# One batch's up-projection and the next attention on TensorE: an order written out by hand

## The chip, the cores and the metric

The kernel runs on one core of a Trainium2 chip. The metric is the device time of one execution in microseconds, the median of several. TensorE (PE in the rows) multiplies matrices; VectorE (DVE), ScalarE (ACT) and GpSimd (POOL) work on elements; SyncE (SP) issues most of the transfers. Each engine takes its instructions in the order that the program gives it.

## The reference

Three layers follow each other. Here they are, cut to what is computed:

```python
def reference(q, k, v, cap, w_in, w_out, w_gate, w1, w2):   # q, k, v: 4 x 12 x 448 x 64
    scores = q @ k.T / 8
    scores = cap * tanh(scores / cap)                       # cap = 30
    attn = softmax(scores) @ v
    x = attn as 1792 x 768                                  # 4 batches of 448 tokens
    g = relu(x @ w_in) ** 2                                 # 768 -> 2048
    x = g @ w_out                                           # 2048 -> 768
    # then each token goes to one of 8 experts, 224 tokens each, by greedy choice on x @ w_gate
    out[tokens of e] = relu(x[tokens of e] @ w1[e]) @ w2[e]
```

The weights w_in and w_out come as 64-bit integers' bits and are decoded on the chip.

## The kernel before, in words

The four batches are worked one after the other, and the attention of a batch runs beside the projections of the batch ahead of it. `merge` takes steps from several generators: each step says how much time it is worth, and the generator that is least far along by its own total goes next. So the program writes down a merged order of `hidden(0)` (up-projection of batch 0) with `attention(1)`; then `output(0)` and `hidden(1)` with `attention(2)`, and so on.

That written order is only a suggestion where a scheduler places the instructions: it may move an instruction ahead of others when its model of the engines finds it ready first. Inside `manual_schedule(engines={PE})` TensorE keeps the written order. Before the change this holds from `attention(2)` on, and not for `attention(0)`, nor for the merge of `hidden(0)` with `attention(1)`.

Attention of a batch goes through six head pairs, 0 to 5. For a head pair there are four blocks of keys: three pairs of 64-row score products (line 233), of which the two halves run at the same time, and one full product (L235). ScalarE takes tanh and exp (L237, L238). The value products are three pairs (L258) and one full product (L261) into one accumulator "aux". The sums of the exponentials, z, are added up block by block (L244, L246, L250): on VectorE for batch 0, on GpSimd for the others. The norm is a pair of products of z with ones (L266); then VectorE adds a small number (L268; ScalarE for later batches), takes the reciprocal (L269) and multiplies (L271), which gives x. `split_rows` splits x in a high part xh (L315, ScalarE) and a low part xl (L316, VectorE).

`hidden` makes 16 tiles of 128 features. A tile is 18 products, three for each of the six head pairs' x: xh with the high weights (L395), xl with the high weights (L396), xh with the low weights (L397). Its accumulator "acc" has two buffers. Behind it ScalarE takes relu, square and a cast (L402 to L406), and VectorE or GpSimd a subtraction (L407). The weights of a tile are loaded, decoded by three VectorE operations (L328 to L330), cast (L356) and split (L357, mostly GpSimd); there are three buffers each for decoded, high and low weights. `output` works alike (L452 to L454).

With `whole` false, attention yields after each group of score or value products, so others may come between them. With `whole` true (batches 2 and 3) a step holds two score blocks, or all value products of a head pair and its norm.

Of the kernel before, what the change touches and what calls it, by code (L numbers as in the profile page):

```python
# [79 lines left out]
class Kernel:  # L80
# [5 lines left out]
    def run(self):  # L86
        tc = self.tc
        PS = bass.MemoryType.PSUM
        with tc.tile_pool(name="keep", bufs=1) as self.keep, \
                tc.tile_pool(name="wts", bufs=1) as self.wts, \  # L90
                tc.tile_pool(name="psum", bufs=2, space=PS) as self.psum, \
                tc.tile_pool(name="dram", bufs=1, space=bass.MemoryType.DRAM) as self.dram, \
                ExitStack() as right, ExitStack() as left:
            self.setup()
            self.mp = right.enter_context(tc.tile_pool(name="moe1", bufs=1, side="right"))
            self.gpool = self.mp
            xs = right.enter_context(ExitStack())
            self.xp = xs.enter_context(tc.tile_pool(name="x", bufs=ND, side="right"))
            with tc.tile_pool(name="x32", bufs=ND, side="right") as self.xq:
                with tc.tile_pool(name="rows", bufs=ND + 1, side="right") as self.tp, \  # L100
                        tc.tile_pool(name="attn", bufs=2, side="right") as self.ap:
                    merge([(self.attention(0), 44.0)])
                    self.split_rows(0)
                    merge([(self.hidden(0), 58.0), (self.attention(1), 44.0)])
                    for b in range(2, NB):
                        self.split_rows(b - 1)
                        streams = [(chain(self.output(b - 2), self.hidden(b - 1)), 118.0), (self.attention(b), 44.0)]
                        if b == NB - 1:
                            streams.append((self.gate_decode(), 30.0))
                        with tc.manual_schedule(engines={mybir.EngineType.PE}):  # L110
                            merge(streams)
                self.split_rows(NB - 1)
            self.gp = left.enter_context(tc.tile_pool(name="gate", bufs=1))
            last = left.enter_context(ExitStack())
            self.gpool = last.enter_context(tc.tile_pool(name="last", bufs=1))
            with tc.tile_pool(name="gate_load", bufs=5, side="right") as self.gl:
                with tc.manual_schedule(engines={mybir.EngineType.PE}):
                    merge([(self.hidden(NB - 1), 60.0), (self.gate_weights(), 80.0)])
            xs.close()
            self.tp = right.enter_context(tc.tile_pool(name="rows2", bufs=2, side="right"))  # L120
            self.rp = right.enter_context(tc.tile_pool(name="route", bufs=1, side="right"))
            self.router_setup()

            def room():
                last.close()
                self.ep = left.enter_context(tc.tile_pool(name="expert", bufs=2))

            with tc.manual_schedule(engines={mybir.EngineType.PE}):
                self.second(room)
# [76 lines left out]
    def attention(self, b):  # L206
# [13 lines left out]
        def load_v(hp):  # L220
            vt[hp] = ap.tile([128, KB + 1, 2 * DH], F32, name="v", bufs=3)
            nc.sync.dma_start(vt[hp], self.v[b, hp])
# [55 lines left out]
        load(0)  # L278
        load(1)
        load_v(0)  # L280
        whole = b > 1
        for hp in range(HP + 1):
            if hp < HP:
                if hp + 2 < HP:
# [613 lines left out]
def merge(streams):  # L898
    live = [[g, 0.0, total] for g, total in streams]
    while live:  # L900
        s = min(live, key=lambda x: x[1] / x[2])
        try:
            s[1] += next(s[0])
        except StopIteration:
            live.remove(s)
# [46 lines left out]
```

## Time and profile before

| | |
|---|---|
| median of 3 runs | 1101.09 us (1098.07 to 1101.76) |
| the profiled execution, its own time | 1098.67 us |
| its span | 1096.8 us |
| TensorE busy with products | 1063.3 us (97%) |
| VectorE busy | 676.2 us (62%) |
| ScalarE busy | 543.8 us (50%) |
| GpSimd busy | 351.0 us (32%) |

A row of the timeline gives the start, the duration, the engine, the line, the operation with its tiles and shapes, and in brackets the idle time ahead of it with what ended it. Products overlap, so the distance from one start to the next tells more than the duration. A 64-row product pair shows as x4, since each fp32 product is recorded in two passes. The granted clock is 1.00 at TensorE's upper level.

### The profile page before, as it was taken

What the parts mean: (1) busy time and instruction counts of PE and PEld (TensorE: products, weight loads), DVE (VectorE), ACT (ScalarE), POOL (GpSimd) and SP (SyncE); (2) the same over time, 40 slices, a digit from 0 to 9 for tenths busy, and PEclk for the clock granted to TensorE, in tenths of its full rate; (3) what the DMA queues carried; (4) which work ended last, traced back from release to release, by engine and by line L of the source; (5) the groups of instructions that cost most, each with busy time, mean ns of one, the idle gap of its engine ahead of it and who ended that gap; (6) DMA issues with size and microseconds to landing.
All of it is one profiled execution on the core that took longest, in us unless ns stands there. A gap on an engine that the chain in (4) does not pass through costs nothing.

```text
span 1096.8 us, 15959 instructions
## 1 busy us (share of the span) xinstructions
PE 1063.3 (97%) x5866; PEld 836.7 (76%) x5866; DVE 676.2 (62%) x1124; ACT 543.8 (50%) x843; POOL 351.0 (32%) x245
## 2 busy tenths in 40 slices
PE   6999999999999999999999999999899999999997
PEld 2336655776677677677787888888799899999996
DVE  5987999978545478788411355565666554555551
ACT  5876776444776744676654222222222223554551
POOL 0127776655221322221443444444210201220000
PEclk9999999999999999999999999999899999999999
DMA  7533655566533377765563233336472465965530
GB/s 278 195 117 124 218 187 203 184 237 232 158 100 95 95 226 245 251 223 200 183 213 95 67 95 103 94 104 213 153 279 70 153 215 179 307 216 185 200 111 26
DMA packets 79454, 187.20 MB, mean 171 GB/s; under 512 B 8528, under 2 KB 19312, under 8 KB 79376
## 3 DMA queue, kind: packets, MB, share of 16 engines
q1 hardware_dynamic: 64736, 169.24, 46.0%
q0 software_dynamic: 3424, 11.19, 3.4%
q10 hardware_dynamic: 11216, 5.75, 2.0%
q8 instruction: 46, 0.75, 0.3%
q14 instruction: 32, 0.26, 0.1%
HBM read 156.26 MB, written 29.88 MB: 170 GB/s over the span
## 4 chain that ended last, share of the span: by engine, by line
PE 65%; issue 12%; DVE 10%; DMA 8%; ACT 2%; POOL 1%; SPq 1%; POOLq 0%; DVEq 0%; ACTq 0%
PE big L877 6%; PE acc L395 6%; PE acc L452 6%; PE acc L396 6%; PE acc L397 6%; PE acc L454 5%; PE acc L453 5%; PE acc L839 5%; PE aux L258 3%; PE big L233 3%; DMA raw<-w_out 3%; PE aux L653 2%; DVE wf L329 2%; DVE wf L328 2%; PE acc L846 2%
## 5 line engine op out<-in xcount | busy, mean ns | idle before, releaser
L356 ACT CAST wh<-wf 128x512 fp32r<-128x512 f32 (+1 forms) x187 | 135.2, 723 | 268.5 <-PE acc L453 102.2
L357 POOL TENSOR_TENSOR wl<-wf,wh 128x512 fp32r<-128x512 f32 (+1 forms) x97 | 156.5, 1616 | 206.5 <-ACT wh L356 196.9
L395 PE MATMUL acc<-xh,wh 128*128 128x448 f32 x384 | 148.6, 389 | 2.0 <-ACT r L402 2.0
L452 PE MATMUL acc<-g,wh 128*128 128x448 f32 x384 | 150.4, 392 | 0.0
L396 PE MATMUL acc<-xl,wh 128*128 128x448 f32 x384 | 141.2, 368 | 1.9 <-DVE xl L316 1.9
L454 PE MATMUL acc<-g,wl 128*128 128x448 f32 x384 | 140.4, 366 | 1.2 <-DVE wl L357 1.2
L397 PE MATMUL acc<-xh,wl 128*128 128x448 f32 x384 | 140.4, 366 | 0.1
L453 PE MATMUL acc<-g,wh 128*128 128x448 f32 x384 | 139.9, 364 | 0.0
L357 DVE TENSOR_TENSOR wl<-wf,wh 128x768 fp32r<-128x768 f32 (+1 forms) x90 | 88.0, 979 | 61.1 <-ACT wh L356 60.3
L877 PE MATMUL big<-wh,g 128*112 128x384 f32 x512 | 117.8, 342 | 0.0
L237 ACT ACTIVATE p<-big,isc 128x896 f32<-128x896 f32 x96 | 85.7, 907 | 26.9 <-PE big L233 26.7
L395 PEld LDWEIGHTS acc<-xh,wh 128*128 128x128 f32 x384 | 72.1, 189 | 35.1 <-issue 15.7
L238 ACT ACTIVATE p<-p,capt 128x896 f32<-128x896 f32 x96 | 89.4, 949 | 1.3
L756 POOL DMA_INDIRECT xg<-x,idx x32 | 34.2, 1068 | 169.9 <-PE acc L775 93.3
L877 PEld LDWEIGHTS big<-wh,g 128*112 128x112 f32 x512 | 86.8, 175 | 0.8
L407 DVE TENSOR_TENSOR g<-r,g 128x448 fp32r<-128x448 f32 x58 | 49.4, 851 | 60.2 <-ACT g L406 57.6
L246 POOL TENSOR_TENSOR z<-z,p 128x896 f32<-128x896 f32 x18 | 38.9, 2162 | 146.4 <-ACT p L238 144.1
L452 PEld LDWEIGHTS acc<-g,wh 128*128 128x128 f32 x384 | 72.4, 189 | 14.4 <-issue 9.6
L396 PEld LDWEIGHTS acc<-xl,wh 128*128 128x128 f32 x384 | 72.6, 189 | 12.4 <-issue 4.1
L269 DVE RECIPROCAL d<-d 128x448 f32<-128x448 f32 x24 | 70.7, 2948 | 16.6 <-ACT d L268 16.5
L233 PE MATMUL big<-qk 64*128 64x448 f32 x288 | 74.1, 598 | 6.9 <-DMA qk<-qk 6.2
L454 PEld LDWEIGHTS acc<-g,wl 128*128 128x128 f32 x384 | 72.0, 187 | 9.4 <-DVE wl L357 2.7
(182 smaller groups left out, 1941.7 us busy)
## 6 DMA issues: line engine op xcount, KB each, us to landing
g<-w SPq DMA_DIRECT2D x68, 384.0 KB
wf<-wi SPq DMA_DIRECT2D x48, 384.0 KB
wf<-wo SPq DMA_DIRECT2D x72, 256.0 KB
wf<-w SPq DMA_DIRECT2D x36, 384.0 KB
raw<-w_in SPq DMA_DIRECT2D x16, 768.0 KB
raw<-w_out SPq DMA_DIRECT2D x24, 512.0 KB
raw<-w_out_t SPq DMA_DIRECT2D x24, 512.0 KB
wt<-wt SPq DMA_DIRECT2D x48, 256.0 KB
```

Of the source, the lines that this page charges most:

```text
L233: nc.tensor.matmul(ps[:, s, :S], k[rows], q[rows], start=True, stop=True)
L237: nc.scalar.activation(p, ps[:, :n, :S], AF.Tanh, scale=self.isc)
L238: e = nc.scalar.activation(p, p, AF.Exp, scale=self.capt)
L356: nc.scalar.copy(wh[:, :w], wf[:, :w])
L357: low.tensor_sub(wl[:, :w], wf[:, :w], wh[:, :w].bitcast(F32))
L395: nc.tensor.matmul(ps, wh[:, d], xh, start=(d == 0), stop=False)
L396: nc.tensor.matmul(ps, wh[:, d], xl, start=False, stop=False)
L397: nc.tensor.matmul(ps, wl[:, d], xh, start=False, stop=(d == ND - 1))
L452: nc.tensor.matmul(ps, a, gh, start=(f == 0), stop=False)
L453: nc.tensor.matmul(ps, a, gl, start=False, stop=False)
L454: nc.tensor.matmul(ps, z, gh, start=False, stop=(f == NF - 1))
L877: nc.tensor.matmul(acc[h][:, s, :DM // 2], l, r[:, s * (DM // 2):(s + 1) * (DM // 2)], start=(j == 0 and first), stop=(j == NF2 - 1 and last))
```

## The change

The merge of `hidden(0)` with `attention(1)` is put inside `manual_schedule` for TensorE, and `whole` becomes true for batch 1 as well.

```diff
                     self.split_rows(0)
-                    merge([(self.hidden(0), 58.0), (self.attention(1), 44.0)])
+                    with tc.manual_schedule(engines={mybir.EngineType.PE}):
+                        merge([(self.hidden(0), 58.0), (self.attention(1), 44.0)])
...
-        whole = b > 1
+        whole = b > 0
```

The new order's line numbers are one higher from line 104 on. The first place is TensorE's order at the end of the first attention. z_335 is the sum of head pair 5, xh_399 and xl_400 are x of head pair 4, xh_403 and xl_404 of head pair 5; acc_455 and acc_530 are tiles 0 and 1 before, acc_457 and acc_532 after; qk_467 and aux_573 belong to the second attention (head pairs 1 and 0). Before:

```order
L266 MATMUL aux_375<-z_335,ones_68 64x448
L395 MATMUL acc_455<-xh_399,wh_419 128x448
L395 MATMUL acc_530<-xh_399,wh_431 128x448
L266 MATMUL aux_375<-z_335,ones_68 64x448
L396 MATMUL acc_455<-xl_400,wh_419 128x448
L397 MATMUL acc_455<-xh_399,wl_420 128x448
L396 MATMUL acc_530<-xl_400,wh_431 128x448
L397 MATMUL acc_530<-xh_399,wl_432 128x448
L233 MATMUL big_544<-qk_467 128x448 x2
L233 MATMUL big_550<-qk_467 128x448 x2
L258 MATMUL aux_573<-p2_478,v_469 64x448 x2
L258 MATMUL aux_573<-p2_484,v_469 64x448 x2
```

And the same place on TensorE in the new order, where qk_467 is head pair 0 of the second attention:

```order
L267 MATMUL aux_375<-z_335,ones_68 64x448
L396 MATMUL acc_457<-xh_399,wh_421 128x448
L267 MATMUL aux_375<-z_335,ones_68 64x448
L397 MATMUL acc_457<-xl_400,wh_421 128x448
L398 MATMUL acc_457<-xh_399,wl_422 128x448
L396 MATMUL acc_457<-xh_403,wh_421 128x448
L397 MATMUL acc_457<-xl_404,wh_421 128x448
L398 MATMUL acc_457<-xh_403,wl_422 128x448
L234 MATMUL big_506<-qk_467 128x448 x2
L236 MATMUL big_513<-qk_467 128x448
L396 MATMUL acc_532<-xh_383,wh_433 128x448
```

Tile 1 has moved behind tile 0, and the second attention's next scores and value products have moved behind the products on x of head pair 5.

The second place is TensorE at the value products of head pair 2 of the second attention, aux_876 before and aux_878 after, with z_695 its sum. Before:

```order
L258 MATMUL aux_876<-p2_712,v_542 64x448 x2
L395 MATMUL acc_866<-xh_395,wh_745 128x448
L396 MATMUL acc_866<-xl_396,wh_745 128x448
L397 MATMUL acc_866<-xh_395,wl_746 128x448
L395 MATMUL acc_866<-xh_399,wh_745 128x448
L396 MATMUL acc_866<-xl_400,wh_745 128x448
L397 MATMUL acc_866<-xh_399,wl_746 128x448
L395 MATMUL acc_866<-xh_403,wh_745 128x448
L396 MATMUL acc_866<-xl_404,wh_745 128x448
L397 MATMUL acc_866<-xh_403,wl_746 128x448
L258 MATMUL aux_876<-p2_810,v_542 64x448 x2
L261 MATMUL aux_876<-p1_816,v_542 128x448
```

And the same place in TensorE's new order:

```order
L259 MATMUL aux_878<-p2_686,v_544 64x448 x2
L259 MATMUL aux_878<-p2_692,v_544 64x448 x2
L259 MATMUL aux_878<-p2_812,v_544 64x448 x2
L262 MATMUL aux_878<-p1_818,v_544 128x448
L267 MATMUL aux_886<-z_695,ones_68 64x448 x2
L396 MATMUL acc_868<-xh_395,wh_758 128x448
```

The projection products no longer stand between the value products, and the norm has moved directly behind them.

The third place is GpSimd's order around the sums of the same head pair, z_715 before and z_695 after; the wl rows split the weights of a tile. Before:

```order
L244 TENSOR_TENSOR z_715<-p2_684,p2_712 128x896
L357 TENSOR_TENSOR wl_627<-wf_578,wh_626 128x768
L407 TENSOR_TENSOR g_667<-r_664,g_667 128x448
L357 TENSOR_TENSOR wl_746<-wf_687,wh_745 128x768
L357 TENSOR_TENSOR wl_794<-wf_737,wh_793 128x768
L246 TENSOR_TENSOR z_715<-z_715,p2_810 128x896
L250 TENSOR_TENSOR z_715<-z_715,p1_816 64x448 x2
```

And in GpSimd's new order:

```order
L245 TENSOR_TENSOR z_695<-p2_686,p2_692 128x896
L358 TENSOR_TENSOR wl_759<-wf_697,wh_758 128x768
L358 TENSOR_TENSOR wl_796<-wf_750,wh_795 128x768
L247 TENSOR_TENSOR z_695<-z_695,p2_812 128x896
L358 TENSOR_TENSOR wl_865<-wf_787,wh_864 128x768
L251 TENSOR_TENSOR z_695<-z_695,p1_818 64x448 x2
```

A weight split has moved in between the last two sums.

## Rows read from the trace of the kernel before

**Rows 1.** Stretches of 20 us: busy time by engine, granted clock, DMA share, GB/s.
```profile
40.00:60.00 20.00, 18.78 (x75) 6.97 (x76) 19.88 (x23) 16.37 (x21) 3.63 (x2) 1.00 0.56 190
60.00:80.00 20.00, 20.00 (x80) 7.36 (x78) 16.16 (x16) 14.40 (x19) 6.52 (x4) 1.00 0.33 111
```
**Rows 2.** Waits of TensorE from 30 to 300 us: us in total, times, longest.
```profile
PE acc L396 <- DVE xl L316: 0.8, 2, 0.5
...
PE aux L266 <- DVE x L271: 0.5, 1, 0.5
```
**Rows 3.** Timeline of TensorE around a lone pair of score products.
```profile
117.58 0.36 PE L396 MATMUL acc<-xl,wh 128*128 128x448 f32 x1
117.78 0.37 PE L397 MATMUL acc<-xh,wl 128*128 128x448 f32 x1
118.08 1.02 PE L233 MATMUL big<-qk 64*128 64x448 f32 x4
119.03 0.47 PE L395 MATMUL acc<-xh,wh 128*128 128x448 f32 x1
```
**Rows 4.** Timeline of TensorE: half pairs, and the first products behind them.
```profile
186.01 1.02 PE L233 MATMUL big<-qk 64*128 64x448 f32 x2
186.95 0.47 PE L452 MATMUL acc<-g,wh 128*128 128x448 f32 x1
187.26 0.37 PE L453 MATMUL acc<-g,wh 128*128 128x448 f32 x1
187.47 0.36 PE L454 MATMUL acc<-g,wl 128*128 128x448 f32 x1
```
**Rows 5.** Timeline of TensorE: a wait, the products behind it, the next attention product.
```profile
102.39 0.60 PE L395 MATMUL acc<-xh,wh 128*128 128x448 f32 x1 [2.05 <-ACT r L402]
102.79 0.57 PE L396 MATMUL acc<-xl,wh 128*128 128x448 f32 x1
...
111.44 1.02 PE L233 MATMUL big<-qk 64*128 64x448 f32 x2
```
**Rows 6.** The stretch behind that wait; the columns are those of rows 1.
```profile
102.00:106.00 4.00, 3.61 (x10) 3.23 (x11) 3.00 (x5) 3.90 (x8) 0.00 (x0) 0.57 0.68 220
```
**Rows 7.** Timeline of VectorE at the end of the first attention.
```profile
70.36 1.26 DVE L250 TENSOR_TENSOR z<-z,p 64x448 f32<-64x448 f32 x2
71.66 0.63 DVE L316 TENSOR_TENSOR xl<-x,xh 128x448 fp32r<-128x448 f32 x1
75.91 0.68 DVE L268 TENSOR_SCALAR d<-aux,eps 128x448 f32<-128x448 f32 x1 [3.63 <-PE aux L266]
76.63 2.95 DVE L269 RECIPROCAL d<-d 128x448 f32<-128x448 f32 x1
79.62 0.62 DVE L271 TENSOR_TENSOR x<-aux,d 128x448 f32<-128x448 f32 x1
81.34 0.63 DVE L316 TENSOR_TENSOR xl<-x,xh 128x448 fp32r<-128x448 f32 x1 [1.10 <-ACT xh L315]
```
**Rows 8.** Timeline of TensorE in the same stretch.
```profile
74.90 0.97 PE L266 MATMUL aux<-z,ones 128*64 128x448 f32 x2
...
76.81 1.77 PE L233 MATMUL big<-qk 64*128 64x448 f32 x8
78.51 2.48 PE L258 MATMUL aux<-p,v 128*64 128x448 f32 x12
...
84.23 0.92 PE L395 MATMUL acc<-xh,wh 128*128 128x448 f32 x2
```
**Rows 9.** Timeline of GpSimd: last sums of a head pair, then a weight split.
```profile
115.99 2.13 POOL L246 TENSOR_TENSOR z<-z,p 128x896 f32<-128x896 f32 x1 [1.44 <-ACT p L238]
118.20 3.16 POOL L250 TENSOR_TENSOR z<-z,p 64x448 f32<-64x448 f32 x2
121.43 2.43 POOL L357 TENSOR_TENSOR wl<-wf,wh 128x768 fp32r<-128x768 f32 x1
```
**Rows 10.** Timeline of VectorE in the first output projection.
```profile
223.62 0.73 DVE L328 TENSOR_SCALAR wf<-raw 128x512 int32<-128x512 int32 x1 [3.96 <-DMA raw<-w_out]
```

## The prediction

> **What bounds the kernel now.** I read the stretches of 20 us first. Between 40 and 60 us VectorE is busy for 19.88 of 20 us and TensorE for 18.78; between 60 and 80 us TensorE is busy for all 20 and VectorE for 16.16 [rows 1]. So the end of the first attention runs at VectorE's pace, and behind it TensorE sets the pace. A busy TensorE can still be slow, because a product that follows another kind starts later; that is read from the distances between starts in TensorE's timeline. Its waits come from the view of waits: two small ones by name in this part, 0.5 and 0.8 us [rows 2], and one of 2.05 us at 102.39 [rows 5].
>
> **The change, part by part.** No product, transfer or vector operation is added or removed. TensorE's order differs only from just before the norm of head pair 2 of the first attention to the first products of the first output projection; before and behind it stands as it was. The other engines keep their work, with some rows exchanged.
>
> *Work on TensorE.* A projection product starts 0.20 us after its forerunner, but the attention product behind it starts 0.30 us later, and a lone pair of 64-row products takes 0.95 us to the next start [rows 3]. Two pairs in one run take 1.70 us (76.81 to 78.51) [rows 8], so a second pair in the run costs 0.75 and a broken run 0.20 more. The first projection product behind attention takes 0.31 us where the later ones take 0.20 to 0.21, and half a pair alone takes 0.94 us, as long as a whole pair [rows 4]. Counted in the two orders over the changed stretch: pairs torn apart go from five to two, 3 x 0.95 = 2.85 us; groups of attention between projection products go from 32 to 26, 6 x (0.10 + 0.10) = 1.2; changes of kind within a group go from 39 to 29, four of them part of the torn pairs, so 6 x 0.10 to 0.20 = 0.6 to 1.2. Sum 4.65 to 5.25. The median distance of each kind of neighbours, applied to both orders, gives 5.0; I take -5.0.
>
> The Trainium skill's page "TensorE: Matmul & The Clock Gate", section "Step-by-step: what each phase is for", says that the drain of one product overlaps the filling of the next, so that the gap is the number of columns and nothing more. By that a change of kind would be free, only the torn pairs would count, and the saving would be 2.85 instead of 5.0. The rows above show 0.30 against 0.20, so the measurement decides here.
>
> *Waits that go.* Before, TensorE stood 2.1 us for a free accumulator (the 2.05 at 102.39), because the relu waited for a subtraction on VectorE. Behind it the products came 0.40 us apart instead of 0.20, at a granted clock of 0.57 [rows 5, 6], which is the lower level, 1.2 GHz, for most of the stretch. The 36 products up to 111.44 took 9.05 us [rows 5]; at 0.20 each with 0.1 at the end they take 7.4, so the low clock cost 1.6. In the new order an attention group stands between tiles 1, 2 and 3, so no two tiles run back to back while the subtractions are late: -2.1 - 1.6. The small waits, 1.3 us, do not go but change place (next part). That is 5.0 us of waits and low clock before.
>
> *A wait that comes.* Before, tiles 0 and 1 of the up-projection advance together, one head pair at a time, as the first attention delivers x. Now tile 1 stands behind all of tile 0 and behind a group of the second attention. Twelve products of tile 1 no longer fill the first attention, 12 x 0.20 = 2.4 us, and joined runs save 0.4 there. VectorE sets the pace until its last sum for head pair 5 ends at 70.36 + 1.26 = 71.6 [rows 7], and none of its work changes, so TensorE's waits up to that point grow from 1.3 to about 4.1. Then the norm of head pair 5 comes at once (71.6 to 73.8: two halves of 0.9 and a projection product between them), and the chain behind it is fixed. From the start of the addition at 75.91 to the end of the subtraction at 81.34 + 0.63 = 81.97 it takes 6.06 us, of which ScalarE's cast was late by 0.5 [rows 7]; so 5.55 us, or 73.9 to 79.4. Before, TensorE covered this chain: from the end of the norm (74.90 + 0.9 = 75.8) to 84.23 it ran four products on head pair 4's x, two score pairs and a whole group of value products [rows 8]. Now only two or three projection products are left (0.5 us), because the next row needs x of head pair 5. TensorE stands for about 4.6 us for its high half and 0.6 for its low half, and tile 0 ends at 80.0. With the 4.1 that makes 9.3 us. The standing is longer than the 2.1 us that lowered the clock before, so I add the same 1.6 us of low clock. Who is queued behind: the whole second attention and all later tiles, since TensorE takes its products in order. The second casts and splits of weights, which wait for tile 0 to end, come some 6 us earlier than before (80.0 against about 86, which is 84.23 and the last products of both tiles), so later weights are not late.
>
> *Norm directly behind the value products.* From the first score of the last two blocks to the norm, the new order has 10.9 us of products (1.5 + 2.3 + 1.8 + 2.0 + 2.4 + 0.9, at the prices above). Before, for such a head pair, the sums on GpSimd ended 9.9 us after that first score (111.44 to 118.20 + 3.16) [rows 5, 9]. So the margin is 1.0 us. For head pairs 2, 4 and 5 GpSimd's order has a weight subtraction of up to 2.4 us between the two sums [rows 9]; then it is 12.3. Pairs 4 and 5 have 12.6 us of products in between, pair 2 has 10.9 and waits 1.4. Bounds: nothing if GpSimd has done the subtraction earlier, 2.4 each for five pairs (12 us) if it never has. I take 0.8, nearer to the low end, since the row's sums of 9.9 fit everywhere but once.
>
> *Sum.* -5.0 - 5.0 + 9.3 + 1.6 + 0.8 = +1.7 us. The profiled execution took 1098.67 us (span 1096.8), 2.4 below the median of the three runs, 1101.09, and within them; by it the time is 1100.4, by the median 1102.8. I put **1101.5**, between the two. What this kernel's measurement can tell from no change is about 0.3%, 3.3 us.
>
> **The rivals.**
> 1. *The wait at tile 0 is mostly covered* (faster). With fewer projection products in the first attention, VectorE's chain itself could move up: its stop of 3.63 us at 75.91 shows that it waited for TensorE there [rows 7]. If x of head pair 5 came 3.6 us earlier, the wait would be 1.6 us without a low clock: 1.7 - 3.6 - 1.6 = -3.5, or 1095.2 to 1097.6 by the two bases. Against it: VectorE stands packed until 72.3 (71.66 + 0.63), whatever TensorE does. It decides from 5.0 us less of waiting and low clock on. Chance 0.25.
> 2. *The norms wait for GpSimd in every head pair* (slower). If the weight subtractions fall between the sums each time, five norms wait 1.5 us each, 7.5 instead of 0.8: +8.4, or 1107.1 to 1109.5; already at 0.5 us each, with the rest as above, it passes 0.3%. For it: the margin of 1.0 us is thinner than one subtraction. Against it: GpSimd's new order has that subtraction in the middle for three pairs only. Chance 0.22.
> 3. *The change does not reach the end* (no change). The first output projection needs weights that VectorE decodes as they land; at 223.62 VectorE stood 3.96 us for such a load [rows 10]. Then a few us won or lost in the changed stretch vanish there, +0.0: 1098.7 to 1101.1. For it: that stop. Against it: TensorE rarely stands there, so the feed only just limits. Chance 0.13.
> 4. *Changes of kind cost nothing* (slower). Then the saving is 2.85 and the sum is +3.85: 1102.5 to 1104.9. The distances in the rows speak against it; chance 0.03. The page named above would have it so.
> My forecast itself, +0 to +3.3: 0.37.
>
> **How the numbers follow.** Faster by over 0.3%: rival 1, 0.25. Within 0.3%: the forecast and rival 3, 0.50. Slower: rivals 2 and 4, 0.25. The likeliest case alone spans 1098.7 to 1104.4 (0 to +3.3 on both bases). The range reaches down to rival 1 with somewhat more of the chain gone, 1094, and up to the lower part of rival 2 (five waits of about 1 us), 1107; beyond it about 0.1 is left out on each side.
>
> **What the changed profile would show.** If I am right: TensorE stands 4 to 5 us before the first product on x of head pair 5, waiting for the cast on ScalarE, near 74 to 79 us, with a granted clock near 0.6 in the four us behind; no wait of 2 us for the relu near 100; value products of a head pair in one run of six, about 2.4 us long, with the norm behind them; and TensorE's first output-projection products within 3 us of where they stood. Wrong would be: products on that x right behind the norm (rival 1), waits of the norm products for sums on GpSimd over 1 us in most head pairs (rival 2), or a difference at the end of the changed stretch that is gone behind the first output projection (rival 3).

## The result, and the profile after

The change made the kernel slower. The median of six runs is 1112.97 us (1108.15 to 1115.98), beside 1101.42 us (1098.07 to 1104.85) for the kernel before in the same comparison: a ratio of 1.0104, with a 95% interval of 1.0081 to 1.0128. The forecast was 1101.5, and its range ended at 1107. The profiled execution took 1112.57 us, its span 1110.8. Lines of the new kernel are one higher from line 104 on.

TensorE's waits in the changed kernel from 40 to 205 us, that is up to product 750 (below), in the first output projection (us in total, times, longest):

```profile
PE acc L396 <- ACT xh L316: 4.4, 1, 4.4
PE aux L267 <- DVE x L272: 3.2, 3, 1.8
PE aux L267 <- DVE z L251: 1.1, 1, 1.1
PE aux L259 <- DVE d L269: 0.6, 1, 0.6
```

Together they are 9.3 us, and the first is the forecast stand for x of head pair 5. In the same view of a longer stretch, 30 to 300 us, there are two more large ones, and both lie further on in that projection, which the forecast had left as it was:

```profile
PE acc L455 <- DVE wl L358: 6.3, 1, 6.3
...
PE aux L431 <- ACT d L269: 1.6, 1, 1.6
```

TensorE's timeline shows both long stands, a stretch at full clock to compare with, and a head pair's value products:

```profile
75.22 0.37 PE L398 MATMUL acc<-xh,wl 128*128 128x448 f32 x1
80.00 0.74 PE L396 MATMUL acc<-xh,wh 128*128 128x448 f32 x1 [4.41 <-ACT xh L316]
...
88.14 1.77 PE L234 MATMUL big<-qk 64*128 64x448 f32 x8
...
101.78 1.02 PE L234 MATMUL big<-qk 64*128 64x448 f32 x4
...
105.51 1.77 PE L234 MATMUL big<-qk 64*128 64x448 f32 x8
...
109.23 2.48 PE L259 MATMUL aux<-p,v 128*64 128x448 f32 x12
111.64 1.02 PE L262 MATMUL aux<-p,v 128*128 128x448 f32 x2
112.59 0.97 PE L267 MATMUL aux<-z,ones 128*64 128x448 f32 x4
...
226.61 0.74 PE L455 MATMUL acc<-g,wl 128*128 128x448 f32 x1 [6.28 <-DVE wl L358]
...
231.98 1.02 PE L234 MATMUL big<-qk 64*128 64x448 f32 x4
```

Tile 0 resumes at 80.00; by the forecast it would have ended there. The value products stand in one run of six with the norm directly behind (109.23 to 112.59), and that norm waits for nothing; in [rows 9] its sum had been the worry. The wait for the relu of [rows 5] is gone: the stretches below show TensorE busy all through 100 to 106 us at full clock. Columns are those of [rows 1].

```profile
78.00:80.00 2.00, 0.00 (x0) 0.00 (x0) 1.34 (x3) 0.56 (x1) 0.00 (x0) 0.50 0.00 0
80.00:82.00 2.00, 2.00 (x5) 1.08 (x7) 0.61 (x1) 0.56 (x1) 0.00 (x0) 0.50 0.00 0
...
86.00:88.00 2.00, 2.00 (x8) 1.65 (x6) 1.97 (x2) 1.09 (x2) 1.96 (x1) 0.63 0.75 232
88.00:90.00 2.00, 2.00 (x11) 0.84 (x10) 1.44 (x1) 0.79 (x1) 1.92 (x2) 1.00 0.03 13
...
100.00:106.00 6.00, 6.00 (x29) 3.97 (x29) 5.83 (x6) 5.49 (x9) 2.34 (x2) 1.00 0.75 248
...
228.00:230.00 2.00, 2.00 (x7) 1.80 (x6) 1.97 (x5) 0.00 (x0) 0.00 (x0) 0.50 0.02 9
230.00:232.00 2.00, 2.00 (x10) 1.54 (x9) 0.41 (x1) 0.62 (x1) 0.93 (x1) 0.79 0.93 298
```

Behind each stand TensorE runs at 0.50, its lower level of 1.2 GHz. What that costs is read from like stretches. From 80.00 to 88.14 there are three projection products, a lone score pair, a full score product and nine projection products. The last three of these groups take 3.73 us at full clock (101.78 to 105.51), and the first about 0.7; 8.14 - 4.4 leaves 3.7 us lost. Behind the second stand, 16 projection products take 5.37 us (226.61 to 231.98) where 3.3 would do, so 2.1 are lost. The Trainium skill's page "TensorE: Matmul & The Clock Gate", section "HAM oscillation — how this bites in real kernels", counts half of the time at the lower level as lost; half of 80.0 to 87.4 is 3.7, so these rows agree with it.

**Where the time goes.** TensorE runs 5866 products in both kernels. Counted in the order of their starts, product 225 starts 12.6 us later than before, product 750 (201.0 us before, in the first output projection) only 4.0 later, product 900 (233.6 before) 13.7, and product 3600 (749.0 before) 11.7. The two orders differ from product 107 to 692, so number 225 is not the same product in both, and 750 and all later numbers are. So most of the first loss is won back, and then 9.7 us are lost in one place, between products 750 and 825. Between products 3600 and 4500, in the routing stage, all profiled executions of other kernels here are 0.6 to 7.7 us slower than the one of before, also where their median is the lower one; so I take this part to belong to that one execution, and compare up to product 3600. There the shift of 11.7 equals the distance of the medians, 11.55.

**The second stand.** VectorE in the changed kernel between the two attentions and in the first output projection, where tiles 16 to 39 are weights of that projection, and L329 to L331 decode one:

```profile
190.93 2.27 DVE L358 TENSOR_TENSOR wl<-wf,wh 128x512 fp32r<-128x512 f32 x1 [1.14 <-ACT wh L357]
193.12 2.94 DVE L270 RECIPROCAL d<-d 128x448 f32<-128x448 f32 x1
195.98 1.03 DVE L329 TENSOR_SCALAR wf<-raw 128x512 int32<-128x512 int32 x1
196.94 2.11 DVE L317 TENSOR_TENSOR xl<-x,xh 128x448 fp32r<-128x448 f32 x2
198.98 2.33 DVE L329 TENSOR_SCALAR wf<-raw 128x512 int32<-128x512 int32 x1
...
202.96 1.28 DVE L331 SCALAR_TENSOR_TENSOR wf<-raw,wf 128x512 int32<-128x512 int32 x2
...
208.76 1.13 DVE L329 TENSOR_SCALAR wf<-raw 128x512 int32<-128x512 int32 x1 [3.98 <-DMA raw<-w_out]
...
217.47 0.43 DVE L329 TENSOR_SCALAR wf<-raw 128x512 int32<-128x512 int32 x1 [1.60 <-DMA raw<-w_out]
...
221.00 0.69 DVE L329 TENSOR_SCALAR wf<-raw 128x512 int32<-128x512 int32 x1 [1.66 <-DMA raw<-w_out]
...
223.07 2.94 DVE L270 RECIPROCAL d<-d 128x448 f32<-128x448 f32 x1
225.93 0.63 DVE L358 TENSOR_TENSOR wl<-wf,wh 128x512 fp32r<-128x512 f32 x1
```

And the same work in the kernel before:

```profile
185.16 0.68 DVE L357 TENSOR_TENSOR wl<-wf,wh 128x512 fp32r<-128x512 f32 x1
185.88 1.24 DVE L328 TENSOR_SCALAR wf<-raw 128x512 int32<-128x512 int32 x1
...
188.49 2.95 DVE L269 RECIPROCAL d<-d 128x448 f32<-128x448 f32 x1
191.35 1.29 DVE L328 TENSOR_SCALAR wf<-raw 128x512 int32<-128x512 int32 x1
...
214.19 0.63 DVE L357 TENSOR_TENSOR wl<-wf,wh 128x512 fp32r<-128x512 f32 x1
```

Before, the decode of tile 21 follows the split of tile 18 at once (185.16 and 185.88) and is done when the last reciprocal of the second attention begins (188.49); tile 22 follows behind it. After, the split of tile 18 itself ends 7.4 us later, at 193.20: VectorE stood 1.14 us for ScalarE's cast, and the split took 2.27 us instead of 0.68. Then the reciprocal stands ahead of both decodes, and splits of x between their first steps; they run mixed and end within a microsecond of each other, the last at 204.24. There are two buffers for raw weights, so two loads go out together, as the queue of transfers shows:

```profile
204.09 0.38 SPq L325 DMA_DIRECT2D raw<-w_out  x1
...
205.01 0.42 SPq L325 DMA_DIRECT2D raw<-w_out  x1
```

VectorE then stands for the first of them until 208.76, and later for two more. Of every six tiles it splits one itself: here tile 24, whose low part stands behind the decodes of tiles 25 and 26 and a reciprocal, in both kernels. It is ready at 226.56 (before at 214.82), and TensorE has stood for it since 220.3, though ScalarE's cast for it was done at 216.6. From the start of the decode of tile 21 to product 750, TensorE was 15.1 us behind before (201.0 - 185.9) and is 9.0 us behind after (205.0 - 196.0): it gains on the decodes by 6 us. Of these, 3.4 are lost when the split of tile 18 ends (7.4 later, where TensorE is 4.0 later), and 2.7 with the reciprocal ahead of the decode. The wait of 1.6 us comes from the same feed: ScalarE's step of L269 (213.75) stood behind a cast that had waited 4.11 us for a decode.

The decode step of 198.98 took 2.33 us where the like one at 217.47 took 0.43. GpSimd was adding sums meanwhile, up to 201.02:

```profile
198.54 2.48 POOL L247 TENSOR_TENSOR z<-z,p 128x896 f32<-128x896 f32 x1 [0.51 <-ACT p L239]
```

The Trainium skill's page "SBUF — State Buffer", section "SBUF: two separate sides", says that VectorE and GpSimd share a pair of ports, and that whichever starts first, a GpSimd instruction or a VectorE one in a 2-port mode or with two inputs in SBUF, holds it for its whole length. If the decode step, which has one input, runs in such a mode, which no run here shows, it would by that end some 0.4 us behind GpSimd's 201.02; it ends at 201.31, so this row agrees.

### The profile page after: what moved, and what is told of

Same layout as the page of the kernel before. It is cut to its first block, busy times and chain, and to the rows that moved or that the text cites. A ratio compares the mean times of both kernels' runs of the same rounds, so it can differ in the third digit from the quotient of the medians.

```text
span 1110.8 us, 15958 instructions
## 1 busy us (share of the span) xinstructions
PE 1064.7 (96%) x5866; PEld 840.9 (76%) x5866; DVE 681.6 (61%) x1124; ACT 544.9 (49%) x843; POOL 352.3 (32%) x245
## 4 chain that ended last, share of the span: by engine, by line
PE 72%; issue 11%; DVE 6%; DMA 5%; ACT 3%; POOL 1%; SPq 0%; POOLq 0%; DVEq 0%; ACTq 0%
PE acc L396 7%; PE acc L453 7%; PE acc L397 7%; PE acc L398 7%; PE big L878 6%; PE acc L455 6%; PE acc L454 6%; PE acc L840 5%; PE aux L259 4%; PE big L234 4%; PE aux L654 2%; PE aux L262 2%; PE acc L847 2%; PE big L236 1%; PE aux L267 1%
## 5 line engine op out<-in xcount | busy, mean ns | idle before, releaser
L358 DVE TENSOR_TENSOR wl<-wf,wh 128x768 fp32r<-128x768 f32 (+1 forms) x90 | 92.0, 1024 | 63.0 <-ACT wh L357 62.1
L878 PE MATMUL big<-wh,g 128*112 128x384 f32 x512 | 120.4, 348 | 0.0
L408 DVE TENSOR_TENSOR g<-r,g 128x448 fp32r<-128x448 f32 x58 | 42.0, 725 | 59.9 <-ACT g L407 57.2
L398 PEld LDWEIGHTS acc<-xh,wl 128*128 128x128 f32 x384 | 72.4, 189 | 6.9 <-DVE wl L358 0.4
```

Source lines behind the costliest of these rows:

```text
L358: low.tensor_sub(wl[:, :w], wf[:, :w], wh[:, :w].bitcast(F32))
L398: nc.tensor.matmul(ps, wl[:, d], xh, start=False, stop=(d == ND - 1))
L878: nc.tensor.matmul(acc[h][:, s, :DM // 2], l, r[:, s * (DM // 2):(s + 1) * (DM // 2)], start=(j == 0 and first), stop=(j == NF2 - 1 and last))
```

## The experiments

**One part alone.** The order alone (e1):

```diff
-        whole = b > 0
+        whole = b > 1
```

> The fixed order alone; the second attention yields after each group as before. Theory A (the order written down costs the time, at both its ends): tile 0 still stands alone behind the first attention, so TensorE waits 4 to 5 us for x of head pair 5 near 80 us and runs at the low clock for about 7 us behind it; the last products of tile 15 still stand behind the first output products, so a wait of 5 to 7 us for split weights comes near 225 us. The torn pairs cost 2 to 3 us more than in the changed kernel: 1111 to 1117 us. Rival B (the grouping costs the time, because sums and norms come in lumps): neither wait, 1100 to 1104 us.

Ratio to the kernel before 1.0097 (1.0065 to 1.0129), no other than the changed kernel's, as theory A had it. Its waits from 30 to 300 us hold both stands, the second just under the 5 us expected:

```profile
PE acc L455 <- DVE wl L358: 4.9, 1, 4.9
PE acc L396 <- ACT xh L316: 4.4, 1, 4.4
```

The grouping alone (e2):

```diff
-                    with tc.manual_schedule(engines={mybir.EngineType.PE}):
-                        merge([(self.hidden(0), 58.0), (self.attention(1), 44.0)])
+                    merge([(self.hidden(0), 58.0), (self.attention(1), 44.0)])
```

> The grouping alone; the order of the first merge is left to the scheduler. Theory A: tiles 0 and 1 advance together beside the first attention, no 4.6 us wait near 80 us and no 6 us wait near 225 us; what is left is the gain on torn pairs and kind changes, up to 5 us less work against the relu wait that comes back: 1096 to 1103 us. Rival B: 1108 to 1114 us, with waits of norms or of weights in the second attention.

Ratio 1.0035 (1.0015 to 1.0056). Neither stand is there, and the wait for the relu is back (2.1 us), as theory A had it; but the time is above what it allowed, 1105.69. TensorE lost 2.4 us up to product 750 without a longer wait. The scheduler tears eight pairs apart there, where the kernel before has five; the three more cost some 2.85 us at 0.95 each, and fewer groups give a part of it back. One of them is a norm's pair, whose halves take 0.9 and 1.0 us:

```profile
144.85 0.96 PE L266 MATMUL aux<-z,ones 128*64 128x448 f32 x2
145.74 0.47 PE L396 MATMUL acc<-xl,wh 128*128 128x448 f32 x1
146.15 0.97 PE L266 MATMUL aux<-z,ones 128*64 128x448 f32 x2
```

So the written order makes both stands, not the grouping (rival B falls).

**The first stand** (e3). The fixed order begins only when tiles 0 and 1 have been written; up to there the scheduler places them beside the first attention, as before:

```diff
+                    rest = merge([(self.hidden(0), 58.0), (self.attention(1), 44.0)], lambda: len(self.G.get(0, ())) >= 2)
                     with tc.manual_schedule(engines={mybir.EngineType.PE}):
-                        merge([(self.hidden(0), 58.0), (self.attention(1), 44.0)])
+                        merge(rest)
...
-def merge(streams):
+def merge(streams, until=None):
...
-    while live:
+    while live and not (until and until()):
...
+    return live
```

> The scheduler still places the merge until two head pairs of the second attention have their scores' groups begun and tiles 0 and 1 are filled beside the first attention; the fixed order begins only then. Theory A1 (the first wait is carried to the end): the 4.4 us wait and most of its low clock go, 6 to 8 us less, and the later wait for split weights stays at 5 to 7 us, since tile 15 is still cut by the boundary: 1105 to 1107 us. Rival C (the feed of the first output projection sets the end whatever TensorE wins ahead of it): the wait near 220 us grows by what was won, 1111 to 1114 us. Rival D (the later wait comes only from TensorE's lateness): it goes as well, 1098 to 1101 us.

Ratio 1.0030 (1.0011 to 1.0049), 1105.22 us, at the lower edge of what A1 expected. Product 750 starts 4.5 us earlier than before, 8.5 earlier than in the changed kernel; the first stand and its low clock are gone. The second is not:

```profile
PE acc L456 <- DVE wl L359: 6.2, 1, 6.2
```

It comes although TensorE is ahead of the kernel before, so lateness doesn't cause it (rival D falls); nor does it grow by what was won (rival C).

**The second stand: is it the boundary between the two orders?** (e4) One fixed order over both merges (the loop over later batches moves into it), so that tile 15 ends ahead of the first output products:

```diff
                     with tc.manual_schedule(engines={mybir.EngineType.PE}):
                         merge([(self.hidden(0), 58.0), (self.attention(1), 44.0)])
-                    for b in range(2, NB):
...
-                        with tc.manual_schedule(engines={mybir.EngineType.PE}):
+                        for b in range(2, NB):
...
                             merge(streams)
```

> One fixed order over both merges, so that the last nine products of tile 15 and the norm of head pair 5 come ahead of the first output products, as written. Theory A2 (the 6.3 us wait for split weights comes from the boundary, which holds tile 15's weight buffers and puts decodes and transfers late): the wait falls under 2 us and with it some 2 us of low clock, 1104 to 1107 us; the first wait near 80 us stays at 4 to 5 us. Rival D (it comes from TensorE's lateness or from where VectorE splits that one tile): the wait stays at 5 us or more, 1110 to 1114 us.

Ratio 1.0086 (1.0057 to 1.0114), and the wait stayed:

```profile
PE acc L455 <- DVE wl L358: 5.5, 1, 5.5
```

I had taken tile 15's held weight buffers for the cause. That theory (A2) falls. The decode of tile 21 starts at 194.71 here, 11.4 us ahead of product 750. What is left of rival D, the place of that one split, comes next.

**Is it the place of one split?** (e5) TensorE's order is untouched; the low part of tile 24 goes to GpSimd.

```diff
-        self.wtile[n] = (wf, w, nc.gpsimd if n >= self.at[NB - 1, "i"] or b == 0 and n % 6 else nc.vector, self.wts, 3)
+        self.wtile[n] = (wf, w, nc.gpsimd if n >= self.at[NB - 1, "i"] or b == 0 and (n % 6 or n == 24) else nc.vector, self.wts, 3)
```

> TensorE's order is that of the changed kernel word for word; only the low split of weight tile 24 goes to GpSimd instead of VectorE, where it stands behind the decodes of tiles 25 and 26 and a reciprocal. Theory E (that place in VectorE's order turns a late transfer into a stop of TensorE): the 6.3 us wait falls under 2.5 us and the low clock behind it goes, 1104 to 1107 us. Rival F (the feed of weights as a whole is late, whoever splits): the wait only moves to another weight and stays at 4 us or more in sum, 1109 to 1113 us.

Ratio 1.0077 (1.0058 to 1.0097). Product 825 starts 4.1 us later than before (13.7 in the changed kernel), so the 6.3 us stand is gone; but product 975 is 10.2 later. The loss has moved to a later split on VectorE and to a stand behind ScalarE, whose casts of late weights hold up its next tanh:

```profile
PE acc L455 <- DVE wl L358: 3.0, 1, 3.0
PE big L234 <- ACT p L238: 2.6, 2, 1.9
```

The wait moved and the time stayed in the range of rival F: the feed as a whole is late.

**Is it the last reciprocal?** (e6) With a total of 50 for the second attention its end stands well ahead of tile 15:

```diff
-                        merge([(self.hidden(0), 58.0), (self.attention(1), 44.0)])
+                        merge([(self.hidden(0), 58.0), (self.attention(1), 50.0)])
```

> The second attention's total is 50 instead of 44, so its steps come earlier in the fixed order and its last norm stands well ahead of the end of tile 15. Theory G (the last reciprocal and the splits of x collide on VectorE with the decodes of tiles 21 and 22, which sets back all later transfers): the collision goes, the wait near 220 us falls under 2.5 us, 1103 to 1107 us; the wait near 80 us stays. Rival F (the feed is late anyway): the wait stays at 4 us or more, 1109 to 1114 us.

Ratio 1.0075 (1.0054 to 1.0097); the wait is 5.5 us. The edit did its part: the x behind that reciprocal is multiplied at 185.71, ahead of tile 18's split at 192.17, and the decode of tile 21 follows soon:

```profile
193.91 0.41 DVE L329 TENSOR_SCALAR wf<-raw 128x512 int32<-128x512 int32 x1
```

That is 11.5 us ahead of product 750 (205.4) instead of 9.0, yet the wait fell only from 6.3 to 5.5 us. So theory G falls: the place of the reciprocal is the smaller part. Two runs (e7, e8) put the last two edits on top of the late start:

> The late start of the fixed order (no stand of 4.4 us near 80 us) together with the low split of tile 24 on GpSimd. If the two waits are the whole loss (theories A1 and E): 1095 to 1100 us, faster than before by 2 to 7 us. If the feed of weights is late whoever splits (rival F): 1102 to 1106 us, no better than the late start alone.

> The late start of the fixed order together with the earlier second attention. If the collision on VectorE at the end of the second attention makes the second wait (theory G): 1094 to 1100 us. If not (rival F): 1102 to 1107 us.

They gave 1.0017 (1.0000 to 1.0034) and 1.0013 (0.9997 to 1.0030), 1104.00 and 1104.69 us: the late start's gain, and little more. In the second the wait is 7.6 us. In the first, product 750 starts 5.0 us ahead of the kernel before, and product 975 1.2 behind: the feed takes back all that was won.

**Is it the transfers?** (e9) Every third tile of the first output projection gets a raw buffer of its own, so that a load goes out one decode earlier:

```diff
-                self.decode(wf, (self.wi if m == "i" else self.wo)[j], w)
+                r = self.wts.tile([128, w], I64, name="raw3", bufs=1) if m == "o" and n % 3 == 1 else None
+                self.decode(wf, (self.wi if m == "i" else self.wo)[j], w, r)
```

> The changed kernel with a third buffer for raw weights of the first output projection (every third tile uses it), so that a load is issued one decode earlier. In the changed kernel VectorE stood 4.0, 1.6 and 1.7 us for such loads between 204 and 221 us, after the decodes of tiles 21 and 22 had ended together. Theory H (these transfers set the feed, and the feed the wait of 6.3 us): VectorE's stops there fall under 2.5 us in sum, TensorE's wait for split weights falls under 1.5 us, 1103 to 1107 us. Rival I (VectorE's own work and the three buffers of decoded weights set the feed): the wait stays at 4 us or more, 1109 to 1113 us.

1107.01 us, ratio 1.0041 (1.0023 to 1.0059): 6.0 us are back, at the upper edge of theory H's range. Its waits of VectorE from 195 to 265 us hold 3.6 us for raw weights (16.1 in the changed kernel), 2.4 of them in the stretch that the expectation names, and TensorE's wait is nearly halved, though not under the 1.5 us expected:

```profile
DVE wf L329 <- DMA raw<-w_out: 3.6, 3, 2.4
```

```profile
PE acc L456 <- DVE wl L359: 3.4, 1, 3.4
```

What is left of it is the place of tile 24's split behind a decode and the reciprocal, which the last run takes away. With the late start (e10):

> The late start of the fixed order with the third raw buffer. Theory H: both losses gone, 1094 to 1100 us. Rival I: 1102 to 1106 us, as the late start alone.

1099.97 us, ratio 0.9980 (0.9960 to 0.9999). The kernel before with the same buffer (e11):

> The kernel before with the third raw buffer, as a control. If the feed was only just enough there, so that its stops for loads cost TensorE nothing (theory H): within 0.3% of the kernel before, 1099 to 1105 us. If the feed held the kernel before back too (rival C): 3 us or more faster, below 1099 us.

1099.54 us, ratio 0.9966 (0.9946 to 0.9987): 3.5 us faster, of which 3 were gained between products 900 and 1125. So the feed held the kernel before back a little as well, beyond its stop in [rows 10]; the run falls at the edge between the two expectations. It also puts e9 in its place: with the buffer in both, the changed order is 7.5 us slower (1107.01 against 1099.54), so of the loss of 11.6 us the buffer takes about 4, and the rest of its 6.0 it gives to the order of before too. With the late start as well (e10) the two are level. Last, the late start, the buffer, and tile 24's split on GpSimd (e12):

> Late start, third raw buffer, and the low split of weight tile 24 on GpSimd. Theory H with E: 1093 to 1099 us, faster than both kernels. Rival I: 1101 to 1105 us.

1096.35 us (1094.38 to 1097.73), ratio 0.9939 (0.9919 to 0.9958): faster than both kernels. TensorE's longest waits from 30 to 300 us are now

```profile
PE big L235 <- ACT p L239: 2.5, 3, 1.0
PE acc L457 <- POOL wl L360: 1.1, 1, 1.1
```

and product 3600 starts 6.4 us earlier than before. Against the same order and split without the buffer (e7, 1104.00) the buffer is worth 7.7 us; against the late start and buffer without the split's move (e10) that move is worth 3.6; alone, in the changed kernel (e5), it brought 2.3, a difference within the noise. Against the control (e11) the late fixed order and the moved split win 3.2 us.

## Why the prediction was wrong

**Up to the first output projection the mechanism was right.** From product 100 (39.3 us in both) to 750 the kernel before takes 161.7 us, the changed one 165.7. The waits of before in it are 3.3 us [rows 2, 5] and its low clock 1.6, which leaves 156.8 of work. After, the waits are 9.3 and the low clock 3.7, which leaves 152.7. So the terms stand thus:

| term | forecast | measured |
|---|---|---|
| work on TensorE | -5.0 | -4.0 (order alone: -2.8) |
| waits and low clock that go | -5.0 | -4.9 |
| waits until tile 0 ends | +9.3 | +9.3 |
| low clock behind them | +1.6 | +3.7 |
| norms waiting for GpSimd | +0.8 | 0 |
| sum | +1.7 | +4.1 |

The mis-sized term is the low clock: "I add the same 1.6 us" took over the price of a 2.05 us stand for one of 4.4. I had the row for the price of each product at the low level, but not for how long it would last. The 3.7 is the highest that was seen: behind the same stand, the same products lost 2.2 to 3.1 us in e1, e4, e5, e6 and e9.

That the waits came to 9.3 is in part luck. Up to the norm they were 4.9 us, where 4.1 had been forecast, and behind it 4.4, where 5.2 had been. "None of its work changes" did not hold: VectorE's last sum for head pair 5 took 3.03 us instead of 1.26, with a sum of GpSimd beside it, and ended at 73.96 instead of 71.6, so half of the norm waited for it.

**What failed is the step that stopped there.** "The other engines keep their work, with some rows exchanged" got no price, and "later weights are not late" was argued from tile 0's buffers alone. At the other end of the changed stretch the decode of tile 21 came 10.1 us later and TensorE only 4.0, and I costed that at nothing without naming what covers it. The cover was TensorE's 15 us behind the decodes, and 9 did not do. That added 7.9 us of waits and 2.1 of low clock. This second stand, and not the low clock of the first, took the time out of the range. Rival 3 had named the place (weights decoded as they land, [rows 10]) but only as something that swallows gains. It could not see that the change itself makes this feed later.

**The rivals.** Rival 1 (the wait mostly covered) and rival 2 (norms waiting in each pair) did not come. Changes of kind were not free (rival 4): the work fell by 4.0 us, where free changes would leave 2.85.

**What stays open.** The runs show that loads issued late, and the place of one split, make the second stand: with the buffer and the moved split it is gone (e12). Why VectorE's decodes come late is not shown. The rows put 3.4 us on the late split of tile 18 and 2.7 on the reciprocal. Where the lead was 11.4 and 11.5 us (e4, e6), the wait was still 5.5 us, and the decode of tile 26 still stood 3.1 us for its load; no run moved the split of tile 18 alone.

## What to carry to other kernels

When an order is fixed for one engine, look at what the scheduler then does with the others at both ends of the stretch, and compare how far the feed of operands is ahead of its user in both; here 6 us of lead were lost with no instruction added. When an experiment removes a wait and the time stays, follow the starts of like-numbered products: they show where it is lost again. Give each mend to the kernel before as well: the three alone gave back 7.8, 2.3 and 6.0 us (e3, e5, e9), and together 16.6 (e12), about their sum, but that is more than the loss of 11.6, since the buffer makes the old order faster too (3.5 us, e11).

## What the hardware showed unexpectedly

The low clock outlasted the stand in front of it: after 4.41 us without a product, TensorE ran at 0.50 until about 87 us, 7 us on. And the same stand need not have the same price: behind 4.41 or 4.42 us and ahead of the same products, the low level ended at 84.3 us in e1 and at 85.0 in e5, and 2.2 and 2.5 us were lost instead of 3.7. Nor does the first row behind a stand tell it. In e9 TensorE waited 3.42 us and its next product shows 0.74 us. In e10 it waited 3.43 us for the same split, and its next product shows 0.47, but from 215.8 on the clock was at 0.50 and the products 0.37 us apart. The price was much the same, some 1.3 us in e9 and 1.6 in e10:

```profile
223.03 0.74 PE L456 MATMUL acc<-g,wl 128*128 128x448 f32 x1 [3.42 <-DVE wl L359]
```

```profile
215.01 0.47 PE L457 MATMUL acc<-g,wl 128*128 128x448 f32 x1 [3.43 <-DVE wl L360]
...
216.04 0.57 PE L455 MATMUL acc<-g,wh 128*128 128x448 f32 x1
216.42 0.57 PE L456 MATMUL acc<-g,wh 128*128 128x448 f32 x1
```
